# Score triangles cut in halves of 32 queries, two quarters sharing one column, in a windowed-attention and MLP-mixer kernel

## The chip, the cores and the metric

The kernel runs on one core of a Trainium2 chip. Its time is the device time of that core in microseconds (us); of several runs the median is given. Engines are named as the profile names them: PE is TensorE (matmuls; PEld its weight loads), DVE is VectorE, ACT is ScalarE, POOL is GpSimd, SP is SyncE, which here only issues DMAs.

## The reference

One block of a network on a sequence of S = 2048 tokens with D = 512 features, all in bfloat16. `c` is a vector of 512; its modulation gives six vectors of 512. Shortened:

```python
sa, ca, ga, sb, cb, gb = (silu(c) @ w_mod).reshape(6, 512)
h = layernorm(x) * (1 + ca) + sa
q, k, v = split(h @ wqkv)                  # 32 heads of 16 features
s = q @ k.T * 16 ** -0.5                   # per head
mask = (i - j >= 0) & (i - j < 256)        # query i, key j
o = softmax(where(mask, s, -1e9)) @ v
x = x + ga * (o @ wo)
h = layernorm(x) * (1 + cb) + sb
u = gelu(layernorm(h).T @ w1 + b1)         # the MLP mixes tokens: 2048 -> 1792
x = x + gb * (u @ w2 + b2).T               # 1792 -> 2048
```

A query sees itself and the 255 keys before it.

## The kernel before, in words

**Groups, units, chunks.** The sequence is worked through in four groups of 512 tokens (G = 0 to 3). A group's tokens are normalized, transposed and projected to queries, keys and values; a group has two halves of 256 queries (`HQ`). A unit is one half with one set of eight heads (`g8`, four sets); there are 32 units. Keys lie in blocks of 64 (`KB`). A half of 256 queries needs four key blocks before it (-4 to -1) and its own four (0 to 3). Key blocks 0 to 3 are each partly cut off by the diagonal, -4 to -1 partly by the window's far edge; in each, one triangle of 64 x 64 is half in use, and the mask sets the other half to zero.

**A chunk** is one set of score banks of 512 columns: PE writes scores of four head pairs side by side into four PSUM banks (`pss` with three, `psb` with one), ACT takes the exponential of both in two instructions (`et`), DVE multiplies the triangles in `et` by a mask (`maskt`). A tuple `(kb, qs, nq, col)` says: key block `kb`, from query block `qs` on, `nq` query blocks, to column `col`. Two units make a pair of five chunks: near and far for the first, one shared chunk with both units' rest (`MID`), near and far for the second. There are 14 pairs, and for the first half of the sequence four chunks `FIRST` and one `MID_FIRST`: 75 chunks in all. When all chunks of a unit are masked, PE forms the sums (`po`): per piece the values (`VT`) and, with a matrix of small constants (`ones_bd`), the denominators. ACT takes the logarithm and the exponential of minus it (`lz`), DVE multiplies (`OT`).

**Heads two by two.** Scores of two heads come out of one matmul: partition 0 to 63 hold 64 keys of the even head, 64 to 127 the same keys of the odd head. For that the keys stand in `KT` twice, each time with the other head's features set to zero (`split`, with `mask_par`), and the values in `VT` in two halves with zeros beside them.

**Values.** In group 0 the value projection writes each parity of heads straight to its partitions, in matmuls of 256 columns (`v` within `proj0`), and a copy with `mask_half` places them. In groups 1 to 3 it is a plain projection; one copy goes to `vb`, two DMAs on SP swap partition halves into `vs` (`e_vx`), and copies of 64 partitions place them in `VT` (`e_vp`, once for its own half, once for the swapped). `VT[1]` is zeroed by a memset at the start, `VT[2]` by two DMAs.

**The order.** Each step is an `Op` with its engine, and `ORDER` lists the 1,165 operations by number in the order of emission; every engine works its share strictly in that order. `CHOSEN` names the engine of those that may run on more than one. PE switches between four score matmuls side by side (tiles of 32 x 128), four narrow ones for sums (128 x 32) and whole ones (128 x 128). `run_schedule` marks dense work that stands close to sums to be done in 128 x 32 as well (`tiled`, through `mm`).

**The rest.** Between the chunks the order puts the projections of the next group, the output projection and normalizations of the last one (`post`), and parts of the token MLP as soon as a group's normalized tokens `hb` are there (`partials`, evicted to `part`). When attention has ended, `tail` does what is left of the first MLP matmul (`pu`, 56 pieces), and the last loop the second one (`py`), with its outputs.

Of the kernel before, what the change touches and what calls it, by code (L numbers as in the profile page):

```python
# [13 lines left out]
P = 128  # L14
S = 2048
# [8 lines left out]
KB = 64  # L24
HQ = 4 * KB
# [91 lines left out]
]  # L117
CHOSEN = {
    "ACT": [
        47, 48, 50, 51, 74, 82, 1062,  # L120
    ],
    "DVE": [
# [5 lines left out]
    ],  # L128
    "POOL": [
# [86 lines left out]
def kernel(  # L216
# [31 lines left out]
    class Ordered:  # L248
        def __init__(self, engine):
            self.engine = engine  # L250

        def __getattr__(self, name):
            call = getattr(self.engine, name)

            def wrapped(*args, **kwargs):
                ins = call(*args, **kwargs)  # L256
                if pinned[0]:
                    tc.keep_in_program_order(ins)
# [1176 lines left out]
```

## Time and profile before

| | |
|---|---|
| median of 3 runs | 253.28 us (252.91 to 253.66) |
| span of the profiled execution, first to last instruction | 252.3 us |
| time of the profiled execution outside its span | not on the page; the median stands 0.98 us above the span |
| PE busy | 235.3 us (93%), 3949 matmuls, 3949 weight loads |
| DVE busy | 205.4 us (81%) |
| ACT busy | 179.5 us (71%) |
| POOL busy | 126.3 us (50%) |
| granted clock of PE | 1.000 |

The page gives for each engine how long some instruction of it ran. Matmuls overlap, and the end of one is modelled, so a busy PE isn't a PE at its full rate. The line of tenths shows how the shares change over the span. In the groups of instructions a row reads: line, engine, operation, output<-inputs, shapes, count | busy us, mean ns of one | idle time before. The program records all through one wrapper, so all rows have line L256, and groups are told apart by the tiles' names. In the timeline a row reads: start us, length us, engine, line, operation, names, shape, count.

### The profile page before, as it was taken

To read this page: it belongs to the slowest core of one execution; us is meant where nothing else is said; L and a number is where in the kernel's file an instruction comes from. 1 tells how busy PE (TensorE), PEld (TensorE's weight loads), DVE (VectorE), ACT (ScalarE), POOL (GpSimd) and SP (SyncE) were. 2 spreads that over 40 slices of the span, in tenths; PEclk is the share of its full clock that TensorE was granted. 3 is DMA by queue.
4 is the path that set the end of the run, shared out by engine and by line. 5 is a ranking of instruction groups with operands and counts; after the bars stand their busy time and mean duration, and the time that the engine had idled before them with its cause. 6 is when DMAs were issued, how large, how long until landed. Compare 5 with 4: busy or idle time off the path is not lost.

```text
span 252.3 us, 9189 instructions
## 1 busy us (share of the span) xinstructions
PE 235.3 (93%) x3949; PEld 126.0 (50%) x3949; DVE 205.4 (81%) x408; ACT 179.5 (71%) x254; POOL 126.3 (50%) x228
## 2 busy tenths in 40 slices
PE   7988888899987889999999999999999999999995
PEld 2656644445554544555546454556444444444443
DVE  5499998989989998999897999999978764444443
ACT  4699998999999999999999999997147510000000
POOL 8268968795899989845886348173000000000000
PEclk9999999999999999999999999999999999999999
DMA  6999364356055200003401536314999201111111
GB/s 200 323 351 294 48 47 86 44 70 187 3 74 112 53 23 3 4 3 104 131 3 45 155 82 189 105 44 113 343 388 386 108 22 43 44 52 52 42 44 42
DMA packets 42625, 28.13 MB, mean 111 GB/s; under 512 B 12376, under 2 KB 38488, under 8 KB 42584
## 3 DMA queue, kind: packets, MB, share of 16 engines
q1 hardware_dynamic: 42576, 27.54, 39.4%
q8 instruction: 31, 0.51, 0.9%
q14 instruction: 10, 0.08, 0.1%
q10 hardware_dynamic: 8, 0.00, 0.0%
HBM read 22.03 MB, written 2.10 MB: 96 GB/s over the span
## 4 chain that ended last, share of the span: by engine, by line
PE 52%; ACT 24%; DVE 7%; DMA 5%; issue 5%; POOL 4%; SPq 1%; POOLq 0%; DVEq 0%
ACT et L256 20%; PE py L256 19%; PE pu L256 16%; PE po L256 5%; PE pss L256 5%; ACT lz L256 3%; PE pa L256 3%; DMA x<-in_A_x_dram 2%; DVE et L256 2%; DMA h1T<-xn 2%; DMA wmod<-in_w_mod_dram 1%; POOL h1T L256 1%; PE pq L256 1%; DVE st L256 1%; PE pk L256 1%
## 5 line engine op out<-in xcount | busy, mean ns | idle before, releaser
L256 ACT ACTIVATE et<-pss 128x1536 bf16<-128x1536 f32 x75 | 110.7, 1476 | 2.8 <-PE psb L256 2.3
L256 PE MATMUL py<-guT,w2r 128*128 128x512 bf16 (+2 forms) x238 | 48.7, 366 | 0.0
L256 ACT ACTIVATE et<-psb 128x512 bf16<-128x512 f32 x75 | 46.9, 626 | 0.0
L256 DVE TENSOR_TENSOR et<-et,maskt 128x1024 bf16<-128x1024 bf16 (+2 forms) x79 | 46.4, 603 | 0.1
L256 PE MATMUL pu<-hb,w1s 128*32 128x512 bf16 (+1 forms) x302 | 39.0, 380 | 0.2 <-DVE QT L256 0.2
L256 PEld LDWEIGHTS <-w2r 128*128 128x128 bf16 x238 | 22.8, 98 | 26.1 <-issue 0.3
L256 PE MATMUL pss<-QT,KT 32*128 32x64 bf16 (+3 forms) x720 | 29.9, 230 | 6.2 <-ACT et L256 3.5
L256 PE MATMUL po<-et,VT 128*32 128x64 bf16 (+3 forms) x960 | 32.2, 234 | 1.3 <-DVE kb L256 0.6
L256 PE MATMUL po<-et,ones_bd 128*32 128x256 bf16 (+3 forms) x624 | 31.7, 268 | 0.0
L256 PEld LDWEIGHTS <-KT 32*128 32x128 bf16 x960 | 17.1, 92 | 28.5 <-issue 24.6
L256 DVE TENSOR_TENSOR otile<-py,xr 128x512 bf16<-128x512 f32 (+2 forms) x17 | 11.2, 660 | 24.4 <-PE py L256 24.2
L256 POOL TENSOR_SCALAR KT<-kb,mask_par 128x512 bf16<-128x512 bf16 (+1 forms) x36 | 25.0, 707 | 11.4 <-DVE kb L256 11.1
L256 PE MATMUL psb<-QT,KT 32*128 32x64 bf16 (+3 forms) x240 | 29.3, 231 | 0.0
L256 PEld LDWEIGHTS <-VT 128*32 128x32 bf16 x960 | 20.8, 96 | 13.2 <-issue 4.7
L256 PE MATMUL pk<-h1T,wqkv 128*32 128x512 bf16 (+4 forms) x228 | 21.1, 340 | 2.4 <-DVE OT L256 1.0
L256 DVE BATCH_NORM_STATS2 st<-x 128x6 f32<-128x512 bf16 x32 | 21.5, 680 | 2.1 <-DMA x<-in_A_x_dram 2.1
L256 PEld LDWEIGHTS <-wqkv 128*32 128x32 bf16 (+1 forms) x350 | 15.3, 96 | 12.7 <-issue 4.7
L256 PEld LDWEIGHTS <-w1s 128*32 128x32 bf16 (+1 forms) x302 | 14.1, 97 | 15.0 <-issue 1.5
L256 PE MATMUL pv<-wqkv,h1T 128*32 128x512 bf16 (+2 forms) x202 | 17.1, 348 | 1.3 <-DVE OT L256 0.7
L256 PE MATMUL pu<-hb,w1r 128*128 128x512 bf16 (+1 forms) x96 | 17.9, 380 | 0.0
L256 PE MATMUL pa<-wod,OT 128*32 128x512 bf16 (+1 forms) x136 | 17.2, 381 | 0.0
L256 PEld LDWEIGHTS <-ones_bd 128*32 128x32 bf16 x624 | 15.8, 97 | 0.1
(109 smaller groups left out, 350.1 us busy)
## 6 DMA issues: line engine op xcount, KB each, us to landing
w2r<-in_B_w_dram SPq DMA_DIRECT2D x14, 512.0 KB, 10.2
w1s<-in_B_w_dram SPq DMA_DIRECT2D x19, 256.0 KB, 4.0
w1r<-in_B_w_dram SPq DMA_DIRECT2D x9, 256.0 KB, 4.3
x<-in_A_x_dram SPq DMA_DIRECT2D x16, 128.0 KB, 5.2
wmod<-in_w_mod_dram SPq DMA_DIRECT2D x4, 512.0 KB, 7.8
out_dram<-otile SPq DMA_DIRECT2D x15, 128.0 KB, 1.7
wmod<-in_w_mod_dram SPq DMA_DIRECT2D x4, 256.0 KB, 3.9
wqkv<-in_A_wqkv_dram SPq DMA_DIRECT2D x4, 256.0 KB, 5.7
```

The lines of the kernel that those rows point to most:

```text
L256: ins = call(*args, **kwargs)
```

## The change

**Half blocks of 32 queries (`QB`).** Pieces are counted in 32 queries instead of 64. The triangles of 64 x 64 are cut where only one half block of queries can see something, so that pieces have 7, 1, 5, 3 or 2 half blocks and the four key blocks of a near or far chunk fill it exactly.

**The shared chunk.** What is left of a unit are, of each of its eight key blocks, 32 queries with 32 keys. For query block `qb` these are the first 32 keys of block `qb` with its first 32 queries (`side` 0) and the last 32 keys of block `qb - 4` with its last 32 queries (`side` 1). The two are now written to different partition halves of the same 32 columns (`score`): 128 columns per unit instead of 256, 256 per shared chunk instead of 512. Both exponentials of it read 256 columns per bank. Its mask runs twice over them: once with one mask into columns 256 to 511, once with the other in place; each pass keeps one side's half of the partitions. The sums of it are eight pieces of 32 columns per unit for the values, and one matmul over 256 columns in a strided view for the denominators.

**Partitions by key half and head.** For this the 128 partitions of a chunk hold: 32 keys even head, the same 32 odd head, the next 32 even, odd. `KT`, `ones_bd`, `mask_half` and the masks follow that layout.

**Values without swaps.** All value projections write with four matmuls of 32 output partitions (`values`), so the DMAs through `vs` go; `place` puts each half into `VT` in one instruction of 128 partitions that writes the zeros too, so the memset and the two DMAs of zeros go. The operations stay in the list as empty ones, so the numbers in `ORDER` keep their meaning. `vb` has three buffers instead of two.

**New order.** `ORDER` is replaced. Counted by its operations: score and other PE work stand in 158 runs of one class instead of 159; changes of tile shape are 162 instead of 158; the first of the scores and the tail begin with the same PE work, one partial-product piece has moved into the tail. `CHOSEN` changes 37 operations: 17 go from DVE to POOL (two `m2`, four `n2`, four `hb`, three `xn`, one `kk`, two `vo`, one `h1T`), 13 from POOL to DVE (four `n2`, two `hb`, one `m2`, two `h1T`, three `vo`, one `vp`), six from DVE to ACT (five evictions `pe` and one `qe`) and one from ACT to DVE (`ke`). In `Ordered` each instruction gets a tie to the one before it on its engine, without a semaphore.

```diff
-FIRST = [(3, 3, 1, 0), (0, 0, 4, 64), (1, 1, 3, 320)]
-NEAR = [(-1, 0, 4, 0), (0, 0, 4, 256)]
-FAR = [(-2, 0, 3, 0), (3, 3, 1, 192), (-4, 0, 1, 256), (1, 1, 3, 320)]
-MID_FIRST = [(2, 2, 2, 0)]
-MID = [(-3, 0, 2, 0), (2, 2, 2, 128)]
+FIRST = [(3, 6, 2, 0), (0, 0, 8, 64), (1, 2, 6, 320)]
+NEAR = [(-1, 0, 7, 0), (3, 7, 1, 224), (-4, 0, 1, 256), (0, 1, 7, 288)]
+FAR = [(-2, 0, 5, 0), (2, 5, 3, 160), (-3, 0, 3, 256), (1, 3, 5, 352)]
+MID_FIRST = [(2, 4, 4, 0)]
...
-        chunks.append((piece_list(a, NEAR), 0, 512, [(192, 128, 1, 512, 0)]))
-        chunks.append((piece_list(a, FAR), 0, 512, [(128, 128, 2, 128, 0)]))
-        chunks.append((piece_list(a, MID) + piece_list(b, MID, 256), 0, 512, [(64, 128, 2, 256, 0)]))
...
+        near, far = [(192, 64, 2, 64, QB)], [(128, 64, 2, 192, QB)]
+        chunks.append((piece_list(a, NEAR), 0, 512, near))
+        chunks.append((piece_list(a, FAR), 0, 512, far))
+        chunks.append(([(a, None, 0, 0, 0), (b, None, 0, 0, 128)], 0, 256, None))
...
-        1: [op("z", "POOL", 3.45, lambda e: po.memset(VT[1][:], 0.0), ready=2.0, pos=-22.0)],
+        1: [op("z", "POOL", 0.0, lambda e: None, pos=-22.0)],
...
+    def values(dst, h1T, tb, n):
+        wv = wqkv[:, :, 2 * D : 3 * D].rearrange("p j (a two d) -> p j two a d", two=2, d=DH)
+        for dc in range(ND):
+            for r in range(4):
+                tok = tb * P + n * KB + r // 2 * QB
+                te.matmul(
+                    dst[QB * r : QB * (r + 1), n, :].rearrange("p (a d) -> p a d", d=DH),
+                    lhsT=h1T[:, dc, tok : tok + QB], rhs=wv[:, dc, r % 2, :, :],
+                    start=(dc == 0), stop=(dc == ND - 1), tile_position=(0, QB * r), skip_group_check=True,
+                )
+
+    def place(eng, dst, src, tb, half):
+        eng.tensor_scalar(
+            out=dst[:, 2 * tb : 2 * tb + 2, :, half * DH : (half + 1) * DH],
+            in0=src[:].rearrange("p i (a d) -> p i a d", d=DH),
+            scalar1=mask_half[:, half : half + 1], scalar2=0.0, op0=ALU.mult, op1=ALU.add,
+        )
...
-            def e_vx(e):
-                vs = box["vs", tb] = work.tile([P, 256], BF, name="vs", tag=vs_tag, bufs=1)
-                dma.dma_start(out=vs[0:KB, :], in_=box["vb", tb][KB:P, 0, :])
-                dma.dma_start(out=vs[KB:P, :], in_=box["vb", tb][0:KB, 1, :])
...
+                for unit, kb, qs, nq, col in pieces:
+                    if kb is not None:
+                        score(unit, kb, QB * qs, QB * nq, col)
+                    else:
+                        for qb in range(4):
+                            for side in range(2):
+                                score(unit, qb - 4 * side, KB * qb + QB * side, QB, col + QB * qb, side)
...
+                if masks is None:
+                    src = et_of[i][:, :, 0:256].rearrange("p j (n s) -> p j n s", s=QB)
+                    for m0, dst in ((0, et_of[i][:, :, 256:512].rearrange("p j (n s) -> p j n s", s=QB)), (3 * QB, src)):
+                        msk = m[:, m0 : m0 + QB].unsqueeze(1).unsqueeze(1).to_broadcast([P, 4, 8, QB])
+                        ve.tensor_tensor(out=dst, in0=src, in1=msk, op=ALU.mult)
+                    return
...
+                if kb is None:
+                    for side in range(2):
+                        for qb in range(4):
+                            value(0, qb - 4 * side, KB * qb + QB * side, QB, col + 256 * side + QB * qb)
+                    for j in range(4):
+                        te.matmul(
+                            unit["ps"][32 * j : 32 * j + 32, 1, :].rearrange("p (b h k) -> p h b k", b=4, h=2),
+                            lhsT=ones_bd[:],
+                            rhs=et_of[c][:, j, :].rearrange("p (h n k) -> p h n k", h=2, k=QB)[:, :, col // QB : col // QB + 4, :],
+                            start=False, stop=True, tile_position=(0, 32 * j), skip_group_check=True,
+                        )
+                    continue
```

More of the change, by code (lines that the diff above doesn't have):

```diff
@@ L24 @@
 KB = 64
+QB = 32
 HQ = 4 * KB
@@ L250, in __init__ @@
             self.engine = engine
+            self.last = None
         def __getattr__(self, name):
@@ L258, in wrapped @@
                     tc.keep_in_program_order(ins)
+                    if self.last is not None:
+                        tc.add_manual_dep(
+                            ins.ins, self.last, mybir.DependencyInfo(mybir.DependencyClass.NoSync, mybir.DependencyReason.DATA),
+                            reason="order",
+                        )
+                    self.last = ins.ins.name
                 return ins
@@ L289 @@
     nc.gpsimd.memset(mask_half[:], 0.0)
-    nc.gpsimd.memset(mask_half[0:KB, 0:1], 1.0)
-    nc.gpsimd.memset(mask_half[KB:P, 1:2], 1.0)
+    for r in range(4):
+        nc.gpsimd.memset(mask_half[QB * r : QB * (r + 1), r % 2 : r % 2 + 1], 1.0)
     modFM = const.tile([P, 8], F32, name="modFM")
@@ L300 @@
     wod = const.tile([P, ND, D], BF, name="wod")
-    maskt = const.tile([P, 3, KB], BF, name="maskt")
+    maskt = const.tile([P, 5, QB], BF, name="maskt")
     ones_bd = const.tile([P, 2 * DH], BF, name="ones_bd")
     nc.gpsimd.memset(ones_bd[:], 0.0)
-    nc.gpsimd.memset(ones_bd[0:KB, 0:DH], ZSCALE)
-    nc.gpsimd.memset(ones_bd[KB:P, DH : 2 * DH], ZSCALE)
+    for r in range(4):
+        nc.gpsimd.memset(ones_bd[QB * r : QB * (r + 1), r % 2 * DH : (r % 2 + 1) * DH], ZSCALE)
     nothing = const.tile([P, D], BF, name="nothing")
@@ L316 @@
     QT = [[kvpool.tile([P, D], BF, name=f"QT{r}_{g}") for g in range(ND)] for r in range(2)]
-    KT = [[kvpool.tile([P, 8, 2, KB], BF, name=f"KT{r}_{g}") for g in range(ND)] for r in range(3)]
+    KT = [[kvpool.tile([P, 8, 2, 2, QB], BF, name=f"KT{r}_{g}") for g in range(ND)] for r in range(3)]
     VT = [kvpool.tile([P, 8, DH, 2 * DH], BF, name=f"VT{r}") for r in range(3)]
@@ L812, in e_v @@
                     box["v", tb] = bank([P, 2, 256], F32, "pv")
-                wv = wqkv[:, :, 2 * D : 3 * D].rearrange("p j (a two d) -> p j two a d", two=2, d=DH)
-                tok = slice(tb * P + n * KB, tb * P + (n + 1) * KB)
-                for dc in range(ND):
-                    for par in range(2):
-                        te.matmul(
-                            box["v", tb][KB * par : KB * (par + 1), n, :].rearrange("p (a d) -> p a d", d=DH),
-                            lhsT=h1T[:, dc, tok], rhs=wv[:, dc, par, :, :],
-                            start=(dc == 0), stop=(dc == ND - 1), tile_position=(0, KB * par),
-                        )
+                values(box["v", tb], h1T, tb, n)
             def e_ve(e):
@@ L828, in e_vp @@
                 for half in range(2):
[L829 to L835 removed]
+                    place(ENGINE[e], VT[0], box["vb", tb], tb, half)
+            vb_tag = turn("vb", 3)
             a, z = dense("v", [0.5] * 2, e_v, hs[tb // 2], pos, cls="V", alloc="od", ready=W_READY[4])
@@ L974, in e_v @@
                 if n == 0:
-                    box["v", tb] = bank([P, D], F32, "pv")
-                for dc in (2 * n, 2 * n + 1):
-                    mm(
-                        box["v", tb][:], h1T[:, dc, tb * P : (tb + 1) * P], wqkv[:, dc, 2 * D : 3 * D],
-                        (dc == 0), (dc == ND - 1),
-                    )
-            def e_ve(e):
-                vb = box["vb", tb] = work.tile([P, 2, 256], BF, name="vb", tag=vb_tag, bufs=1)
-                copy(
-                    e, vb[:].rearrange("p two (a d) -> p a two d", d=DH),
-                    box["v", tb][:].rearrange("p (a two d) -> p a two d", two=2, d=DH),
-                )
-            def e_vx(e):
-                vs = box["vs", tb] = work.tile([P, 256], BF, name="vs", tag=vs_tag, bufs=1)
-                dma.dma_start(out=vs[0:KB, :], in_=box["vb", tb][KB:P, 0, :])
-                dma.dma_start(out=vs[KB:P, :], in_=box["vb", tb][0:KB, 1, :])
-            def e_vp(e, own):
-                for half in range(2):
-                    rows = slice(KB * half, KB * half + KB)
-                    block, src = (half, box["vb", tb][rows, half, :]) if own else (1 - half, box["vs", tb][rows, :])
-                    ENGINE[e].tensor_copy(
-                        out=VT[r3][rows, 2 * tb + block, :, half * DH : (half + 1) * DH],
-                        in_=src.rearrange("p (a d) -> p a d", d=DH),
-                    )
-            vb_tag, vs_tag = turn("vb"), turn("vs")
+                    box["v", tb] = bank([P, 2, 256], F32, "pv")
+                values(box["v", tb], h1T, tb, n)
+            def e_ve(e):
+                box["vb", tb] = work.tile([P, 2, 256], BF, name="vb", tag=vb_tag, bufs=1)
+                copy(e, box["vb", tb][:], box["v", tb][:])
+            vb_tag = turn("vb", 3)
             war = [av_ops[G - 2, g] for g in range(ND)] if G >= 2 else []
@@ L1008, in v @@
             a.frees = [ve_op]
-            vx = op("vx", "SP", 1.05, e_vx, deps=[ve_op], pos=pos, extra=0.1)
-            own = op("vo", {"POOL": 0.78, "DVE": 0.45}, 0.78, lambda e: e_vp(e, True), deps=[ve_op] + war + zeros[r3], pos=pos)
-            b = op("vp", {"POOL": 0.78, "DVE": 0.45}, 0.78, lambda e: e_vp(e, False), deps=[vx] + war + zeros[r3], pos=pos)
-            slot(vb_tag, ve_op, own, vx)
-            slot(vs_tag, vx, b)
-            v_done[G, tb] = [own, b]
+            vx = op("vx", "SP", 0.0, lambda e: None, deps=[ve_op], pos=pos, extra=-2.0)
+            placed = [
+                op(("vo", "vp")[half], {"POOL": 0.78, "DVE": 0.45}, 0.78,
+                   lambda e, half=half: place(ENGINE[e], VT[r3], box["vb", tb], tb, half), deps=[ve_op] + war, pos=pos)
+                for half in range(2)
+            ]
+            slot(vb_tag, ve_op, *placed)
+            v_done[G, tb] = placed
         for n, pos in sorted(p_at.items(), key=lambda f: f[1]):
@@ L1168, in e_s, with score @@
                 box["sb", i] = ps_b.tile([P, D], F32, name="psb")
[L1169 to L1172 removed]
+                def score(unit, kb, q, width, col, side=None):
+                    block = 4 * unit["H"] + kb
+                    own = KT[block // 8 % 3][unit["g8"]]
+                    q += (unit["H"] % 2) * HQ
+                    part = slice(0, P) if side is None else slice(KB * side, KB * (side + 1))
                     for j in range(4):
                         rows = slice(32 * j, 32 * j + 32)
[L1175 removed]
+                        dst = box["sa"][part, j, col : col + width] if j < 3 else box["sb", i][part, col : col + width]
                         te.matmul(
[L1177 to L1180 removed]
+                            dst, lhsT=own[rows, block % 8, :, :, :] if side is None else own[rows, block % 8, side, :, :],
+                            rhs=QT[unit["G"] % 2][unit["g8"]][rows, q : q + width],
+                            start=True, stop=True, tile_position=(32 * j, part.start), skip_group_check=True,
+                        )
+                for unit, kb, qs, nq, col in pieces:
[5 more added lines that the diff above has]
+                                score(unit, qb - 4 * side, KB * qb + QB * side, QB, col + QB * qb, side)
             def e_ea(e, i=i, lo=lo, hi=hi):
```

90 lines of the change are left out of this document (40 added, 50 removed), and 123 rows, old and new, of tables (CHOSEN, ORDER).

## The prediction

> **What bounds the kernel now.** The page first: its head, the row of busy times, and the busy tenths in 40 slices of 6.3 us.
>
> ```profile
> span 252.3 us, 9189 instructions
> PE 235.3 (93%) x3949; PEld 126.0 (50%) x3949; DVE 205.4 (81%) x408; ACT 179.5 (71%) x254; POOL 126.3 (50%) x228
> PE   7988888899987889999999999999999999999995
> DVE  5499998989989998999897999999978764444443
> ACT  4699998999999999999999999997147510000000
> ```
>
> The slices show two regimes. From slice 2 to slice 27 ScalarE (ACT) is full and VectorE (DVE) nearly so; after that ACT is almost empty and TensorE (PE) alone is full. The shares of the whole span (PE 93%, ACT 71%) hide this, so the second view is the table of windows, cut where the timeline has the first score matmul (10.78 us) and the end of the last group of sums (174.75 us). I call the first row the attention stage, the second the tail.
>
> ```profile
> 10.78:174.75 163.97, 151.94 (x3518) 87.06 (x3517) 153.42 (x300) 160.53 (x219) 119.26 (x201) 1.00 0.39 92
> 174.75:252.30 77.55, 74.73 (x366) 34.41 (x358) 46.58 (x90) 13.49 (x24) 0.00 (x0) 1.00 0.38 134
> ```
>
> Columns: length, busy PE, PEld, DVE, ACT, POOL, granted clock, DMA share, GB/s. In the stage ACT is busy 160.53 of 163.97 us, 98%; DVE 94%; POOL 73%; the clock is 1.00 throughout. The view of waits agrees: who waits for scores or for ACT's reading of them waits little, because the two keep each other just fed.
>
> ```profile
> PE pss L256 <- ACT et L256: 3.5, 12, 0.5
> ACT et L256 <- PE psb L256: 2.3, 5, 0.7
> POOL VT L256 <- DMA vs<-vb: 3.0, 2, 2.3
> ```
>
> So the stage is ACT's, and the tail is a fixed string of PE work. PE's busy time in the stage is no measure of its need. Rows of the timeline give that:
>
> ```profile
> 169.47 0.39 PE L256 MATMUL po<-et,ones_bd 128*32 128x256 bf16 x8
> 169.87 0.26 PE L256 MATMUL pss<-QT,KT 32*128 32x192 bf16 x3
> ...
> 169.95 0.21 PE L256 MATMUL pss<-QT,KT 32*128 32x64 bf16 x3
> ...
> 169.98 0.21 PE L256 MATMUL pss<-QT,KT 32*128 32x64 bf16 x3
> ...
> 170.01 0.26 PE L256 MATMUL pss<-QT,KT 32*128 32x192 bf16 x3
> ...
> 170.21 0.41 PE L256 MATMUL po<-et,VT 128*32 128x192 bf16 x16
> ...
> 178.34 1.89 PE L256 MATMUL pu<-hb,w1s 128*128 128x512 bf16 x8
> ```
>
> Four score matmuls lie side by side in the array. A 192-column group is followed after 0.08 us, which is 2.4 columns per ns; the 64-column groups follow after 0.03 us. The last group starts at 170.01, streams 0.08 us, and the sums start at 170.21: 0.10 to 0.12 us are lost where the shape of the tiles changes. Counting the stage's work in columns at 2.4 per ns, four narrow ones side by side: scores 75 x 512 (16.0 us), sums 76,800 (32.0), 32 value, 62 key and query, 56 partial-product, 28 output-projection and 8 modulation pieces of 1,024 columns or the same in quarters (186 x 0.427 = 79.4). Sum 127.4 us. The order has some 156 changes of tile shape in the stage; at 0.10 us they are 15.6 us. PE needs 143 us of the 164; some 21 us of its stage is waiting, most of it covered by the modelled ends.
>
> **ACT.** The change halves the columns of the 14 shared chunks (the third of each pair's five): the exponentials read 768 and 256 columns instead of 1,536 and 512.
>
> ```profile
> L256 ACT ACTIVATE et<-pss 128x1536 bf16<-128x1536 f32 x75 | 110.7, 1476 | 2.8 <-PE psb L256 2.3
> L256 ACT ACTIVATE et<-psb 128x512 bf16<-128x512 f32 x75 | 46.9, 626 | 0.0
> L256 ACT ACTIVATE lz<-po 128x256 f32<-128x256 f32 x32 | 13.0, 405 | 0.7 <-PE po L256 0.5 <-DVE OT L256 0.2
> L256 ACT ACTIVATE part<-pu 128x512 f32<-128x512 f32 x1 | 0.6, 600 | 0.0
> ```
>
> The two exponentials give (1476 - 626) / 1024 = 0.83 ns per column; the 256-column row (405 against 414 by that slope) says that the slope holds down there. 1,024 columns less are 0.85 us a chunk, 14 x 0.85 = 11.9 us less. The new assignment brings five evictions of partial products to ACT (5 x 0.60 = 3.0 us); a key copy leaves and a query copy comes, which cancel. ACT's stage: 160.5 - 11.9 + 3.0 = **151.6 us**.
>
> **DVE.** Masks: before, 43 of 1,024 elements and 32 of 512. After, the far chunks' 28 shrink to 512, and the 14 shared chunks take two passes of 1,024 (an upper copy into the empty half, then the lower in place): 29 of 1,024 and 60 of 512. That is 28 x 456 - 14 x 742 = +2.4 us; the rows are of runs of 64 and 128 elements, and runs of 32 are not shown: between no more and, if the rate halved, 50 us x 0.6 = 30 us; I take the rows, to which the new runs are nearest in kind: each is still contiguous.
>
> ```profile
> L256 DVE TENSOR_TENSOR et<-et,maskt 128x1024 bf16<-128x1024 bf16 x43 | 31.8, 742 | 0.1
> L256 DVE TENSOR_TENSOR et<-et,maskt 128x512 bf16<-128x512 bf16 x32 | 14.3, 456 | 0.0
> L256 DVE COPY part<-pu 128x512 f32<-128x512 f32 x13 | 8.8, 678 | 0.3 <-PE pu L256 0.2
> L256 DVE TENSOR_TENSOR h<-h,bc_sb 128x512 bf16<-128x512 bf16 x12 | 6.0, 500 | 0.4
> L256 DVE TENSOR_TENSOR h<-h,bc_cb 128x512 bf16<-128x512 bf16 x12 | 5.4, 448 | 0.9 <-POOL h L256 0.8
> L256 DVE TENSOR_SCALAR hb<-h,rs,nm 128x512 bf16<-128x512 bf16 x4 | 2.5, 627 | 0.0
> L256 DVE TENSOR_SCALAR h<-x,rs,nm 128x512 bf16<-128x512 bf16 x4 | 2.0, 497 | 0.0
> L256 DVE TENSOR_SCALAR xn<-x,rs,nm 128x512 bf16<-128x512 bf16 x3 | 1.9, 631 | 0.0
> L256 DVE TENSOR_SCALAR h1T<-h1T,modFM 128x512 bf16<-128x512 bf16 x4 | 1.5, 426 | 0.0
> L256 DVE TENSOR_SCALAR KT<-kb,mask_par 128x512 bf16<-128x512 bf16 x2 | 1.0, 526 | 0.0
> L256 DVE COPY VT<-vb 64x256 bf16<-64x256 bf16 x4 | 0.9, 216 | 0.0
> ```
>
> The new assignment moves to POOL two modulations of two instructions (2 x 0.95), four hb (2.5), three xn (1.9), four n2 (2.0), one key split (1.05), two value placements (4 x 0.216), one h1T (0.85): 11.1 us off; to ACT the five evictions, 3.4 off. It takes from POOL four n2 (2.0), two hb (1.25), one modulation (0.95), two h1T (1.7), and four value placements, each now one pass of 512 like the split's 526 (2.1): 8.0 on. DVE's stage: 153.4 + 2.4 - 14.5 + 8.0 = **149.3 us**.
>
> **POOL and DMA.** Values now reach both halves of the partitions from TensorE, so 24 swaps through SyncE (48 small DMAs) and the two zero-filling DMAs go, and each placement is one instruction.
>
> ```profile
> L256 POOL COPY VT<-vs 64x256 bf16<-64x256 bf16 x24 | 10.8, 452 | 3.9 <-DMA vs<-vb 3.0
> L256 POOL COPY VT<-vb 64x256 bf16<-64x256 bf16 x20 | 10.2, 511 | 3.5 <-DVE vb L256 2.9
> L256 POOL TENSOR_SCALAR VT<-vb,mask_half 128x512 bf16<-128x512 bf16 x8 | 5.8, 731 | 1.3 <-DVE vb L256 1.3
> L256 POOL MEMSET VT<- 128x4096 bf16 x1 | 3.5, 3517 | 0.1
> ```
>
> 44 copies (21.0 us) become 20 passes of 731 ns (14.6); values aside, 15 operations come from DVE and 9 go to it; six more at 731 ns a pass, one or two passes each, are 4 to 9 us. POOL stays near 119 us of the stage; the 45 us in which it is idle there hide this, and without them the 4 to 9 us would show. The memset that goes (3.5 us) pays for more mask building before the stage. What the 3.0 us of waits for swaps covered is late for nobody: the next wait of POOL is for DVE's value copy.
>
> **PE.** The shared chunk's scores become 64 matmuls of 32 columns in 32x64 tiles, its sums 64 of 32 columns plus 8 of 256; the near chunks get two 32-column pieces each in scores and in sums. With w for one row of four tiles of 32 columns (eight half-wide ones for scores), a pair has 8 steps in the shared scores, 16 in the shared sums and 8 in its near chunks, 32, where before the same work was 512 + 512 + 256 columns, 0.533 us. No row shows 32 columns. From below the column rate gives w = 0.013: 32 x 0.0133 - 0.533 = -0.11 us a pair, -1.5 us in all. From above, a load that hides behind nothing:
>
> ```profile
> L256 PEld LDWEIGHTS <-VT 128*32 128x32 bf16 x960 | 20.8, 96 | 13.2 <-issue 4.7 <-DVE QT L256 0.6
> ```
>
> w = 0.096 gives 2.54 us a pair, +36 us. I take w = 0.03, the 64-column groups, nearest in size and with the same loads, hidden there: 0.43 us x 14 = +6.0 us. The value projections keep their columns. The near sums now also wait for the values of blocks 3 and -4, which the far sums right behind them waited for before, and all sums of a unit start when its three masks are done: nothing. Changes of tile shape go up by four (+0.4), one partial-product piece moves to the tail (-0.4). PE needs 143 + 6 = **149 us**.
>
> A second row bears on w, matmuls of one single column, eight of which start 0.025 us apart ((0.34 - 0.163) / 7, the end being that of one):
>
> ```profile
> 6.06 0.34 PE L256 MATMUL ps_fm<-sT,wmod 128*128 128x1 bf16 x8 [0.43 <-DVE sT L256]
> L256 PE MATMUL ps_fm<-sT,wmod x32: 163/163/177, 6.1 to 7.6; 128*128 128x1 bf16 x32
> ```
>
> The Trainium skill, "TensorE: Matmul & The Clock Gate", section "Wait — 56ns, not 53.3ns?", says that starts never come closer than about 25 ns however few the columns; by that rule, an estimate from the page, the term would be +3.7 us instead of +6.0, and the row with its 25 ns agrees.
>
> **The sum.** Three engines that needed 160.5, 153.4 and 143 now need 151.6, 149.3 and 149. If ACT kept its 98% the stage would be 154.9. Three nearly equal engines with buffers between them will hardly do that; I take 97%, 156.5 us, 7.5 less than 164.0. With 0.4 more in the tail the span is 245.2. The page gives the span alone; the median of the runs, 253.28, stands 1.0 above it, so **246.2 us**.
>
> **The rivals.** *PE takes over* (loads partly shown, w of 0.04 to 0.05): 32 x 0.04 - 0.533 = 0.75 us a pair, PE at 153.5, and at 97% a stage of 158; at 0.05 1.07 us, 158 and 163: 248 to 252.7 us. For it: 32-column loads come twice as thick as any in the profile. Against: in the 64-column rows four loads of 96 ns fit in 0.03 us. The Trainium skill, "TensorEngine Tiling (Array Packing)", section "Restrictions and Gotchas", says that column tiling shuts off the fast load, which would strike the 32x64 scores. Here such a load is bounded by the 96 ns row over two buffers, 0.05.
>
> *Slower: the weight loads don't hide at all.* The place is the shared chunk's sums and scores, the price w = 0.096, 36 us on PE; PE at 179, and 179 / 0.97 is a stage of 184: 274 us. It decides from w about 0.052, where PE reaches 159 and the whole gain is gone. Against it speak the same rows.
>
> *The order eats it*: DVE, at 94% of the stage before, stays at 94%, as every mask, copy and normalization waits in its one queue: 149.3 / 0.94 = 158.8, or with the mask runs 10% dearer (+5) 164: 248.5 to 254 us.
>
> *The columns don't bind*: the exponentials shrink but the stage keeps its 164 us, because chunks are paced by the copies and sums between them: 253.5. Against: ACT has 3.4 us of idle time in the stage.
>
> **How the numbers follow.** Chances: forecast 0.70 (241.3 to 249.5), PE takes over 0.10, order 0.11, no effect 0.03, slower by loads 0.06. A measurement of this kernel tells about 0.3% (0.8 us) from nothing. Faster: 0.70, most of PE's and of the order's cases: 0.84. Same 0.05; slower 0.11. The range: below, ACT at 99% gives a stage of 153.1 and 242.8 us, and the same with the five evictions in ACT's idle time 150.1 and 239.8; I go halfway, 241.3. Above, to the order's and PE's cases, 252.
>
> **What would show it.** The 14 shortened exponentials at about 840 and 415 ns; ACT's stage near 152 and still the fullest; 32-column groups 0.025 to 0.03 us apart; masks at 456 and 742 ns; the end of the sums at 167 to 168 us and a tail of 78 us. PE rows full with ACT waiting for scores, or 32-column groups over 0.05 us apart, would prove me wrong.

## The result, and the profile after

The changed kernel takes 278.28 us (275.96 to 278.98, 4 runs), the kernel before 253.47 us beside it: a ratio of 1.0965 [1.0917, 1.1014]. It is 25 us slower, where 7 us faster was forecast, and 26 us above the end of the range. Medians and ratios here and below leave out the few executions that ran in the chip's slower state. The page of the kernel after, its head, busy times, tenths and instruction packets:

```profile
span 276.6 us, 13144 instructions
PE 249.5 (90%) x5955; PEld 142.9 (52%) x5955; DVE 213.8 (77%) x410; ACT 174.7 (63%) x259; POOL 128.0 (46%) x226
PE   7999889879977899786998999897799999999996
DVE  4599999988989979597877999986875985533543
ACT  4599997888978679793988789896513760000000
q8 instruction: 46, 0.75, 1.1%
```

ACT, which was at 9 nearly all through the stage, is mostly at 7 to 9 now; its work has shrunk, the stage hasn't. PE has 2,006 more matmuls and as many more weight loads. The last line had been this in the page before:

```profile
q8 instruction: 31, 0.51, 0.9%
```

These packets are the program itself, 16 KB each (0.75 MB in 46). PE's matmuls and loads number 11,910 here and 7,898 before, which is 259 and 255 for each packet; I take a packet as 256 of PE's instructions. The table of windows of after, the attention stage and the tail (columns as in the prediction; this stage, and those of e9, e13 and e17 further down, are cut 0.3 us ahead of their first score and last sum):

```profile
11.72:196.89 185.17, 164.77 (x5521) 103.18 (x5522) 162.49 (x304) 155.19 (x224) 121.86 (x184) 0.99 0.29 72
196.89:276.58 79.69, 75.30 (x375) 34.67 (x363) 46.36 (x89) 13.98 (x24) 0.00 (x0) 1.00 0.35 126
```

The stage has grown from 164.0 to 185.2 us, and none of the five engines is full in it; the tail is 2 us longer (one stop of 1.8 us lies there, the `pu` row below). So the loss is a matter of waiting, and the view of waits of after says whose:

```profile
ACT et L254 <- PE psb L254: 14.6, 26, 3.8
ACT lz L254 <- PE po L254: 10.6, 12, 2.1
PE po L254 <- issue: 7.5, 9, 1.5
PE pv L254 <- issue: 4.5, 4, 2.9
PE pu L254 <- issue: 1.8, 1, 1.8
PE pss L254 <- issue: 1.7, 3, 0.9
```

ACT waits for PE (14.6 us for scores, 2.3 before; 10.6 for sums, 0.5 before), and PE waits for "issue", that is for nothing that the profile shows. The view of before has no such row for PE. One of these stops in the timeline of after:

```profile
121.77 0.40 PE L254 MATMUL po<-et,VT 128*32 128x32 bf16 x32
122.00 0.31 PE L254 MATMUL po<-et,ones_bd 128*32 128x256 bf16 x4
122.11 0.63 PE L254 MATMUL pv<-wqkv,h1T 128*32 128x256 bf16 x16
122.67 0.20 PE L254 MATMUL pss<-QT,KT 32*64 32x32 bf16 x3
...
123.15 0.20 PE L254 MATMUL psb<-QT,KT 32*64 32x32 bf16 x1
123.28 0.50 PE L254 MATMUL pv<-wqkv,h1T 128*32 128x256 bf16 x9
126.65 0.43 PE L254 MATMUL pv<-wqkv,h1T 128*32 128x256 bf16 x7 [2.87 <-issue]
```

The nine and the seven are one operation of 16 like matmuls with no wait between them; PE stands in the middle of it for some 3 us. The windows around it:

```profile
119.00:123.00 4.00, 4.00 (x169) 2.65 (x168) 4.00 (x6) 3.91 (x6) 3.84 (x5) 1.00 0.48 140
123.00:127.00 4.00, 1.13 (x48) 0.58 (x46) 2.18 (x4) 1.58 (x4) 3.45 (x4) 0.99 0.24 63
127.00:131.00 4.00, 4.00 (x113) 2.17 (x110) 3.84 (x5) 1.94 (x2) 3.01 (x3) 0.59 0.02 4
```

In the first PE takes 337 instructions in 4 us, 84 per us. In the packets' own records of this trace no two start closer than 3.35 us, at the median they are 3.80 us apart (6.1 before): 256 instructions in 3.35 us are 76 per us at best. A packet came here at 124.09 and had landed at 125.14; the one before it had started at 116.64. By the starts of its instructions PE stands 21 times in the stage for over 0.4 us with no semaphore to wait for, 20.4 us together, and 20 of these stops end 1.26 to 1.56 us after a packet has landed. Before, there is none.

The count of instructions agrees. Up to the stop shown, the trace has 6,840 matmuls and loads of PE, which is 26 x 256 + 184, and the packet that lands during this stop is the 26th. The other 19 stops that end behind a packet come at 256 times the number of packets landed by their end, plus 184 to 188. So PE stands each time at the same place of a packet, and goes on once the next has landed. This is the theory that the runs test: **PE runs out of instructions**. The rival theories are those of the prediction (loads that don't hide, the order, DVE).

### The profile page after: what moved, and what is told of

Its sections match the earlier page's. It is cut to its first block, busy times and chain, and to the rows that moved or that the text cites. A ratio compares the mean times of both kernels' runs of the same rounds, so it can differ in the third digit from the quotient of the medians.

```text
span 276.6 us, 13144 instructions
## 1 busy us (share of the span) xinstructions
PE 249.5 (90%) x5955; PEld 142.9 (52%) x5955; DVE 213.8 (77%) x410; ACT 174.7 (63%) x259; POOL 128.0 (46%) x226
## 4 chain that ended last, share of the span: by engine, by line
PE 74%; DVE 10%; issue 7%; ACT 5%; DMA 2%; SPq 1%; DVEq 0%
PE pu L254 18%; PE py L254 17%; PE po L254 12%; PE pss L254 10%; ACT et L254 5%; PE pa L254 4%; PE pv L254 4%; DVE et L254 4%; PE pk L254 3%; PE pq L254 3%; DMA wmod<-in_w_mod_dram 2%; DVE QT L254 1%; DVE h L254 1%; PE psb L254 1%; DVE OT L254 1%
## 5 line engine op out<-in xcount | busy, mean ns | idle before, releaser
L254 ACT ACTIVATE et<-pss 128x1536 bf16<-128x1536 f32 (+1 forms) x75 | 100.1, 1334 | 18.2 <-PE psb L254 14.6
L254 DVE TENSOR_TENSOR et<-et,maskt 128x512 bf16<-128x512 bf16 (+2 forms) x93 | 55.4, 611 | 2.6 <-ACT et L254 2.1
L254 PE MATMUL po<-et,VT 128*32 128x32 bf16 (+5 forms) x1856 | 37.9, 200 | 7.7 <-issue 5.3
L254 ACT ACTIVATE et<-psb 128x512 bf16<-128x512 f32 (+1 forms) x75 | 41.8, 557 | 0.0
L254 PEld LDWEIGHTS <-KT 32*128 32x128 bf16 (+1 forms) x1856 | 23.7, 98 | 27.7 <-issue 25.1
L254 PE MATMUL pss<-QT,KT 32*64 32x32 bf16 (+7 forms) x1392 | 35.1, 203 | 3.0 <-issue 1.7
L254 PE MATMUL psb<-QT,KT 32*128 32x224 bf16 (+3 forms) x464 | 34.4, 204 | 0.6 <-issue 0.6
L254 POOL TENSOR_SCALAR VT<-vb,mask_half 128x512 bf16<-128x512 bf16 x28 | 22.6, 814 | 10.5 <-DVE vb L254 10.5
L254 PE MATMUL pv<-wqkv,h1T 128*32 128x256 bf16 x512 | 18.4, 274 | 4.6 <-issue 4.5
L254 ACT ACTIVATE lz<-po 128x256 f32<-128x256 f32 x32 | 12.3, 388 | 10.9 <-PE po L254 10.6
```

## The experiments

All were timed against the kernel before on the same chip, whose median there was 253.6 to 254.0 us. I give the median and the ratio. The cuts of code are shortened, and some of their lines say in words what the edit does.

### Which part of the change

**e1**: after, but the chunks of the pairs in the form of before.

```diff
-near, far = [(192, 64, 2, 64, QB)], [(128, 64, 2, 192, QB)]   # and a shared chunk of 256 columns
+NEAR64, FAR64, MID64 in pieces of 64 queries, a shared chunk of 512 columns
```

> All of the changed kernel but its half-block pieces: near, far and shared chunks are cut in blocks of 64 queries as before, shared chunks have 512 columns again. PE has 8,328 instructions (7,900 before, 11,912 changed). Supply (PE stops inside unreleased runs because its instructions come at most 256 in about 3.5 us): the stops of over 0.4 us within a run go, some 31 to 33 instruction packets, 251 to 259 us, ACT again fullest. Order (the new order and assignment lose the time): still 270 us or more. Narrow steps (32-column pieces cost array time beyond their count): 250 to 256 us, as for supply.

260.09 us, 1.0234 [1.0194, 1.0273], with 32 packets: 1 us above the range of supply and 10 us below that of the order.

**e5**: after with the `ORDER` and `CHOSEN` of before.

```diff
-ORDER, CHOSEN = those of after
+ORDER, CHOSEN = those of before
```

> The changed kernel with the order and the assignment of the kernel before: half-block triangles and value projections without swaps stay. 12,104 PE instructions. Supply: no order helps, 275 to 285 us with 46 or 47 packets. Order (the new order or assignment costs the 25 us): 250 to 256 us.

274.85 us, 1.0829 [1.0764, 1.0894], with 47 packets: at the lower end of what supply gave, far from the order's range.

**e6**: both edits of e1 and e5, which leaves the layout and the values without swaps.

> The changed kernel with the order and assignment of before and with triangles of 64 as before: what is left of the change is the partition layout and the values without swaps. 8,520 PE instructions, 33 packets. Supply: enough time for them at some 5.5 us a packet, 252 to 256 us. If the values in quarters cost by themselves: 257 us or more.

253.27 us, 0.9982 [0.9958, 1.0006], with 33 packets. The four corners: the half blocks cost 18 us in the new order (260.1 to 278.3) and 22 in the old (253.3 to 274.9); the new order 7 and 3 us; layout and values nothing that can be told. The loss is the half blocks'.

**e11**: e1 with the engines (`CHOSEN`) of before.

> The changed kernel with triangles of 64 and the engine assignment of before, but the new order: tells the two apart in the 6.8 us between the run with triangles of 64 (260.1) and the run with values alone (253.3). If the assignment costs it (3 us more on ACT, which is full with triangles of 64): 254 to 256 us. If the order: 259 to 262 us.

271.46 us, 1.0682 [1.0611, 1.0754]. Neither expectation holds: the new order with the old engines is 11 us worse than with its own. Order and assignment are one thing here and can't be split.

### Instructions or columns

**e2**: after, its dense work never in quarters (`NEAR_RUN` 7 to 0). **e3**: e2, and the value projections of groups 1 to 3 in whole matmuls. Both keep every piece of 32 columns and take other instructions away.

```diff
-NEAR_RUN = 7
+NEAR_RUN = 0
```

> The changed kernel with dense work never cut in quarters: 672 PE instructions fewer (11,240), all 32-column pieces kept, more changes of tile shape (some 40 at 0.1 us). Supply: 2.6 packets of 256 fewer at 3.6 us each, less the added shape changes: 268 to 274 us. Narrow steps or order: 278 us, or up to 4 us more for the shape changes.

> As the kernel with whole dense work, and the value projections of groups 1 to 3 in four whole matmuls of 512 columns in place of 32 of 256 in quarters; the values then lie in another layout, the work of all other engines is the same. 10,568 PE instructions, 1,344 fewer than the changed kernel, all 32-column pieces kept. Supply: 5 packets fewer, 258 to 266 us. Narrow steps or order: 276 to 282 us.

273.74 us, 1.08 [1.0753, 1.0848], with 44 packets; 266.38 us, 1.0498 [1.0443, 1.0553], with 41. The first lies in supply's range, the second 0.4 us above it, and both outside those of the rivals. Two packets less are 4.5 us, three more 7.4: 2.3 to 2.5 us a packet, and the 32-column pieces are all still there.

**e4, e8**: the kernel before with each score and sum matmul cut into pieces of at most 64, and of at most 128 columns. The same columns, masks, exponentials and order; 67 and 43 packets.

```diff
-te.matmul(dst[:, col : col + n], ...)
+for o in range(0, n, 64): te.matmul(dst[:, col + o : col + min(o + 64, n)], ...)
```

> The kernel before with every score and sum matmul cut into pieces of 64 columns: the same columns in the same order, 17,212 PE instructions instead of 7,900, no piece narrower than those it already had. Supply: about 16,500 instructions in the attention stage, 64 packets of 256 at 3.5 us, 226 us instead of 164: 300 to 320 us. Narrow steps: the 64-column groups ran at 0.028 us for 0.0267 us of columns, some 3 us more: 255 to 258 us. Order: 253 to 256 us.

> The kernel before with every score and sum matmul cut into pieces of at most 128 columns: same columns, same order, 11,004 PE instructions, no piece narrower than 64. Supply: some 10,300 in the stage are 40 packets, 141 us at 3.5 us each, under 164 us on the whole but over it where sums crowd: 256 to 272 us, with stops inside unreleased runs. Otherwise: 253 to 255 us.

355.63 us, 1.4006 [1.3965, 1.4046], and 261.72 us, 1.0312 [1.025, 1.0374]. e8 is where supply put it; e4 went far above what I expected. Its page and its waits:

```profile
PE 269.4 (76%) x8605; PEld 154.3 (44%) x8605; DVE 206.4 (58%) x408; ACT 185.4 (52%) x254; POOL 121.2 (34%) x228
q8 instruction: 67, 1.10, 1.3%
PE po L256 <- issue: 45.6, 28, 4.2
PE pss L256 <- issue: 11.3, 7, 2.4
```

PE waits 57 us for "issue" in two rows where the kernel before has none. The clock may have a part in the rest: its mean was 0.932 in the trace of e4, against 0.988 in after and 1.000 before; how much of the 102 us that makes is not shown. No piece is of 32 columns and no tile of 32 x 64 here, so neither form is needed for the loss; many instructions are enough.

**e9**: after with the shared chunk in few instructions. The scores run in 16 matmuls of 64 columns instead of 64 of 32, the value sums in 16 of 128 instead of 64 of 32 (the keys met are then wrong ones); exponentials, masks, order and the rest are those of after.

```diff
-for qb in range(4):
-    for side in range(2):
-        score(unit, qb - 4 * side, KB * qb + QB * side, QB, col + QB * qb, side)
+for qb in (0, 2):
+    score(unit, qb, KB * qb, KB, col + QB * qb)
...
-for qb in range(4):
-    value(0, qb - 4 * side, KB * qb + QB * side, QB, col + 256 * side + QB * qb)
+value(0, -4 * side, 128 * side, 128, col + 256 * side)
```

> The changed kernel, order and all, with the shared chunk's matmuls widened: its scores in 16 matmuls of 64 columns instead of 64 of 32, its value sums in 16 of 128 instead of 64 of 32. It leaves out the right keys for these scores and sums; columns read by ACT, masks, copies and everything else are the same. 9,224 PE instructions instead of 11,912. Supply: 36 packets, the stops inside runs shrink to a few us, and what is left is the forecast's sum without its missing term: 246 to 254 us. If something else in the change cost the time (masks, new order): above 262 us.

253.99 us, 0.9998 [0.9961, 1.0036], 36 packets: 24 us of the 25 are back, for ten packets again 2.4 us each. The 32-column pieces of the near chunks have stayed.

**e7, e10**: e6 with four of the pairs in half blocks, which stays within the supply on average, and the same with `NEAR_RUN` 0.

> As the kernel with values alone, but four of the 14 pairs (numbers 1, 3, 5, 7) in half-block form, no two of them neighbours: 9,544 PE instructions, 37 packets, exponentials shorter by 4 x 0.85 = 3.4 us. Supply: a pair of 10.9 us then has room for three packets, so the extra one of a pair mostly hides: 249 to 254 us. If half-block work costs in proportion whatever the supply (narrow steps): 4/14 of 25 us more, 258 to 262 us.

> As the kernel with four pairs in half-block form under the old order, with dense work never cut in quarters: 8,680 PE instructions instead of 9,544, some 40 more changes of tile shape at 0.1 us. Supply: 3.4 packets fewer near their limit give 3 to 6 us, the shape changes take 2 to 4 back: 252 to 257 us. If supply doesn't bind at four pairs: 258 to 260 us.

256.25 us, 1.0101 [1.0037, 1.0164], and 258.77 us, 1.0213 [1.014, 1.0285]. Both are above what I expected. In e10 fewer packets (34 against 37) did not help. My reading, which no run shows alone: with the supply no longer short, the changes of tile shape that `NEAR_RUN` saves cost more. A mixture brings nothing.

### Where the forecast gain went

e9 is all but fed (two stops that end behind a packet are left in its stage, 2.2 us together), but it is level with before, not 7 us faster. Its stage and the change from the second to the third group, in the views of windows, groups, and timeline (PE, then DVE, then POOL):

```profile
10.31:174.27 163.96, 151.04 (x4152) 94.04 (x4178) 156.66 (x304) 152.12 (x224) 120.77 (x184) 0.99 0.31 83
80.00:84.00 4.00, 1.26 (x64) 1.02 (x59) 3.93 (x8) 1.51 (x2) 1.92 (x3) 1.00 0.62 160
84.00:88.00 4.00, 4.00 (x99) 2.37 (x92) 4.00 (x8) 2.62 (x4) 4.00 (x5) 0.57 0.02 6
L254 DVE TENSOR_TENSOR et<-et,maskt 128x1024 bf16<-128x1024 bf16 x29 | 23.8, 820 | 0.5
82.81 0.29 PE L254 MATMUL po<-et,VT 128*32 128x128 bf16 x8 [2.74 <-DVE OT L254]
77.91 1.26 DVE L254 TENSOR_TENSOR h<-h,bc_sb 128x512 bf16<-128x512 bf16 x1
79.09 1.37 DVE L254 TENSOR_TENSOR h<-h,bc_cb 128x512 bf16<-128x512 bf16 x1
80.50 1.25 DVE L254 TENSOR_TENSOR h<-h,bc_sb 128x512 bf16<-128x512 bf16 x1
82.35 0.41 DVE L254 TENSOR_TENSOR OT<-po,lz 128x256 bf16<-128x256 f32 x1
77.67 1.22 POOL L254 TENSOR_TENSOR h<-h,bc_sb 128x512 bf16<-128x512 bf16 x1
78.85 1.34 POOL L254 TENSOR_TENSOR h<-h,bc_cb 128x512 bf16<-128x512 bf16 x1
80.26 1.21 POOL L254 TENSOR_TENSOR h<-h,bc_sb 128x512 bf16<-128x512 bf16 x1
```

DVE is the fullest now, 156.66 of 163.96 us. For 2.74 us up to 82.81 PE stands, waiting for an `OT` that is queued on DVE behind these modulations; ACT has 1.5 us of work in four; and the granted clock is 0.57 in the 4 us after. The modulations take 1.25 to 1.37 us on DVE while POOL runs the same kind beside it; the prediction quoted 448 and 500 ns for them. Three theories for the missing gain: DVE's time, PE's own work, or the fixed order with its changes of group.

**e12**: e9 without the second of the two mask passes of a shared chunk (14 x 820 ns less on DVE; wrong keys stay in its lower quarters). **e16**: e12 without one of the four matmuls in each projection of the later groups (part of the sum is missing).

```diff
-for m0, dst in ((0, upper), (3 * QB, src)):
+for m0, dst in ((0, upper),):
```

> As e9 (the changed kernel with the shared chunk in 24 instructions instead of 128), and without the second of the two mask passes of a shared chunk, the one in place: the lower quarters keep the scores of a few wrong keys. 14 passes of 1,024 elements at the 820 ns of e9 are 11.5 us less on DVE; PE and ACT have the work of e9. Theory (once PE is fed, DVE is the bound, busy 157 of e9's 164 us of the stage): DVE falls to 145.6, ACT with 152.4 becomes the fullest, at 97% a stage of 157 and a time of 246 to 249 us. Rival (what is left of the stops between packets, or the chain of scores, exponentials and sums, holds the stage): 252 to 255 us, as e9, with DVE idle more.

> The changed kernel with its shared chunk in few instructions and one mask pass (e12), and the projections of the groups after the first without one of their four matmuls, as in e14: about 8 us less on PE and some 400 instructions fewer, so two packets fewer. If PE's own work and supply hold the relieved changed kernel: 244 to 248 us. If the order (waits of several engines for one another) holds it: 250.5 to 253.5 us.

252.92 us, 0.9946 [0.9914, 0.9977], and 252.63 us, 0.9934 [0.9901, 0.9967]. The mask passes taken from DVE bring some 1 us, which the intervals of e9 and e12 hardly tell from nothing, the 8 us of PE nothing that can be told: both go to the rival. (The shared chunk has 32 score and value matmuls in these kernels, where the expectation says 24.)

**e13, e14, e15, e17, e18** take work from the kernel before, in its own order: from ACT (the forecast's very saving, the shared chunk's exponentials over 256 columns), from PE (the projections as in e16), from both, from ACT and DVE, from DVE (the shared chunk's mask cut to 16 columns).

```diff
+if masks == [(64, 128, 2, 256, 0)]:            # e13, e15: ACT
+    hi, masks = 256, 2 * [(64, 128, 1, 256, 0)]
...
-for dc in (2 * n, 2 * n + 1):                  # e14, e15: PE
+for dc in ((2, 3) if n else (0,)):
...
-[(64, 128, 2, 256, 0)]                         # e17 (with hi = 256), e18: DVE
+[(64, 16, 1, 256, 0)]
```

> The kernel before with less work for ACT alone: the two exponentials of each of the 14 shared chunks read 768 and 256 columns instead of 1,536 and 512, the shared masks run twice over these 256 columns in the two passes of 512 elements (so DVE has 2.4 us more, as in the changed kernel), and the sums read the first 256 columns twice; the scores of the other half are left unused. PE's work and its instructions are those of before. Theory 1 (the forecast's: ACT alone bounds the stage): ACT falls by 11.9 us, the stage to about 155 at 97%, a time of 243 to 248 us. Theory 2 (PE is as full as ACT, its waits are covered by nothing): 250.5 to 254 us, with ACT idle in waits for scores.

> The kernel before with less work for PE alone: of the four matmuls of 512 columns in each query, key and value projection of the groups after the first one is left out (that part of the sum is missing). About 38 pieces at 0.213 us are 8 us less on PE. Theory 1 (ACT alone bounds): 252 to 254 us. Theory 2 (both are full, neither has slack): 250 to 253.5 us, the ACT waits for scores gone. If PE alone were the bound: 245 to 247 us.

> The kernel before with both reliefs, ACT's of e13 and PE's of e14. Theory 1 (ACT alone bounds): as e13, 243 to 248 us, no lower than it by more than a microsecond. Theory 2 (both are full): 243 to 248 us, at least 4 us below e13 and below e14. If DVE holds the stage at its 94% (153.4 + 2.4 us): 251 to 254 us.

> The kernel before with less for ACT, as in e13, and less for DVE: of the mask of each of the 14 shared chunks only 16 of its 256 columns are run (the rest keeps the scores of wrong keys), some 14 x 0.65 = 9 us less on DVE than before. Theory 1 (DVE's one queue, full at 94%, paces the stage, and ACT right behind it): 244 to 248.5 us, at least 4 us below e18. Theory 2 (the order and the changes of group hold the time, whatever engine is relieved): 251 to 255 us, with the stop of PE and ACT near 80 us still there.

> The kernel before with less for DVE alone, as in e17 (about 9 us), and ACT's work as before, 160.5 us in the stage. Theory 1 (DVE and ACT bound it together): 250.5 to 253 us, held by ACT. If DVE alone paced it: 245 to 249 us. Theory 2 (the order): 252 to 255 us.

| work taken from | us | ratio |
|---|---|---|
| ACT (e13) | 256.93 | 1.0109 [1.0054, 1.0165] |
| PE (e14) | 254.04 | 0.9998 [0.9969, 1.0027] |
| ACT and PE (e15) | 256.52 | 1.0114 [1.0045, 1.0183] |
| DVE (e18) | 252.51 | 0.9950 [0.9930, 0.9969] |
| ACT and DVE (e17) | 250.45 | 0.9865 [0.9834, 0.9896] |

Theory 1 of e13, the forecast's own, is not met: with ACT's stage down from 160.5 to 150.6 us the kernel is 3 us slower. But this isn't ACT's relief alone, as DVE has 157.7 us in the stage instead of 153.4, and theory 2's 254 us is exceeded too. e14 lies at the upper edge of theory 1, and e15 fits none of its theories. The stage and the change of group in e13, with three masks of DVE there, then the stages in e17 and in e18 and the change of group in e17:

```profile
11.98:178.57 166.59, 153.44 (x3517) 87.26 (x3518) 157.69 (x315) 150.59 (x220) 119.35 (x201) 0.99 0.35 88
80.00:84.00 4.00, 1.68 (x53) 1.48 (x56) 4.00 (x6) 2.35 (x4) 3.84 (x5) 0.83 0.53 125
84.00:88.00 4.00, 4.00 (x84) 1.78 (x80) 3.90 (x8) 1.88 (x4) 3.88 (x6) 0.74 0.35 93
78.43 3.58 DVE L256 TENSOR_TENSOR et<-et,maskt 128x512 bf16<-128x512 bf16 x3
```

```profile
10.57:170.93 160.36, 150.59 (x3517) 86.39 (x3518) 146.81 (x301) 149.61 (x220) 115.38 (x201) 1.00 0.40 94
10.76:172.80 162.04, 151.45 (x3519) 87.25 (x3519) 147.20 (x300) 160.27 (x219) 115.20 (x201) 1.00 0.39 94
80.00:84.00 4.00, 3.64 (x100) 1.83 (x103) 3.81 (x9) 3.17 (x5) 3.88 (x7) 1.00 0.33 92
```

In e13 DVE is full at the same place, PE and ACT stand, and the clock falls again. Three of its masks of 512 take 3.58 us there, 1.2 us each, with modulations of POOL beside them; the row of before has 456 ns. In e17 ACT and DVE have 149.6 and 146.8 us of work, yet the stage is 160.4: 11 us less on the fullest engine and 7 less on the second bring 3.2 us, between the two theories' ranges.

Two pairs of these runs differ in one relief alone. e18 and e17 have DVE alike (147.2 and 146.8 us): 11 us less on ACT bring 2.1 us. e13 and e17 have ACT alike (150.6 and 149.6 us): 11 us less on DVE bring some 6 us. So neither engine holds the kernel before by itself. Once ACT is relieved, DVE's queue takes the gain away, and with both relieved most of the forecast's gain is still missing. What keeps it is not settled: PE, with its 150.6 us, was not relieved in e17, the stop at 80 us that theory 2 named isn't there (PE is busy for 3.64 of the 4 us), and no run changed the order at 80 us alone. None of the kernels that do all the work is faster than the kernel before; e6 is level with it.

## Why the prediction was wrong

**ACT: right.** The rows of after:

```profile
L254 ACT ACTIVATE et<-pss 128x768 bf16<-128x768 f32 x14 | 11.4, 811 | 5.3 <-PE psb L254 5.1
L254 ACT ACTIVATE et<-psb 128x256 bf16<-128x256 f32 x14 | 5.3, 378 | 0.0
L254 DVE TENSOR_TENSOR et<-et,maskt 128x1024 bf16<-128x1024 bf16 x29 | 26.7, 921 | 0.5
L254 DVE TENSOR_TENSOR et<-et,maskt 128x512 bf16<-128x512 bf16 x60 | 28.3, 483 | 2.1 <-ACT et L254 2.1
L254 PE MATMUL po<-et,VT 128*32 128x32 bf16 x1120 | 18.5, 178 | 5.2 <-issue 4.2 <-DVE OT L254 1.0
```

811 and 378 ns against 840 and 415. ACT's stage is 155.2 us in after and 152.1 in e9, against 151.6.

**DVE: mis-sized.** It has 162.5 us in after and 156.7 in e9, against 149.3. The masks are 26.7 + 28.3 = 55.0 us instead of 48.9, and the modulations dearer too. It isn't the runs of 32: the two passes of 1,024 with nothing beside them on POOL take 689 ns (678 before). The 20 that have POOL's one-input work beside them for over half their time take 945. Above the fastest of its own form each, DVE's two-input work (the TENSOR_TENSOR rows) took 7.7 us more before, 19.4 in after, 14.3 in e9. With the order and the engines of before it is 10.7 (e5), so most of the rise came with the new ones. The assignment that I counted as 11.1 us off DVE put on POOL what slows DVE.

The Trainium skill, "SBUF — State Buffer", section "SBUF: two separate sides", says that a DVE operation with two inputs from SBUF and a GpSimd operation that reads SBUF lock a shared pair of ports against each other. The rows of e9 agree for DVE: its modulations take 1.25 to 1.37 us beside POOL's, and 0.42 alone. For POOL they show little: its modulations take 1.21 to 1.34 us beside those, and 1.16 the one time that DVE has no two-input operation beside it.

**PE: the step that failed.** I turned the whole risk into w, the time of a step of 32 columns. For the sums w was right: the 32 matmuls from 121.77 to 122.00 us are eight steps of 0.029 us, against 0.03. For the shared scores it was half of what a step took: 64 matmuls take 122.67 to 123.15, 0.48 us, against 0.24, which is 3.4 us over 14 chunks. But the term that decided was not in the sum at all: the change brings 4,012 matmuls and loads more, and their supply has a rate. In the stage alone it cost 20 us of stops, and with fewer instructions 24 of the 25 us came back (e9). I had "32-column loads come twice as thick as any in the profile" in front of me and asked only whether they hide, not whether they arrive. *The weight loads don't hide at all* gave 274 us, near the measurement for a reason that isn't the one: a step of w = 0.096 is not there.

**The sum: also failed.** A stage at 97% of its fullest engine was not reached by any kernel in which ACT has the forecast's saving: e9 has 95.5%, e17 93%. (151.6 / 0.97 is 156.3 us, not 156.5.) *The order eats it* gives the stage of 164 us that e9 has, with dearer masks as it says; but 9 us less on DVE bring only some 1 us (e12), so DVE's queue alone doesn't explain it. And "the stage is ACT's" was wrong for before: ACT is 98% busy, yet 11 us less of it are worth 2.1 us (e18 against e17). A count was wrong too, without weight in the sum: the swaps that go are 24 DMAs on the page, not 48.

**The signs.** ACT waiting for scores came, 14.6 us of it, but beside a PE that stands, not one that is full. "32-column groups over 0.05 us apart" came for the shared scores (0.06 us a step of eight) and not for the sums (0.029). 167 to 168 us for the end of the sums is 197.

## What to carry to other kernels

Count a change's instructions per engine, not only its columns and bytes: on PE, where a matmul brings its load with it, hold the count in each stretch against the rate at which instruction packets come, and look for "issue" waits in the middle of like matmuls. An engine at 98% did not hold the time alone where a second one was at 94% in a fixed order: take its work away by itself first and see. When work is moved to POOL, ask what DVE does beside it.

## What the runs showed of the hardware

- Instructions come to PE in packets of 256, never closer than 3.35 us in after and 3.8 us at the median there. Beyond some 75 per us (256 in 3.35 us) PE stands, up to 4.2 us at a time (e4), and in after it did so 20 of 21 times at the same place of a packet. The Trainium skill, "Runtime: NRT & Kernel Launch", section "Instruction fetch mechanics", has the 16 KiB blocks of 256 instructions, and calls the cost of crossing them "mostly hidden". Here it was 20 us in the stage of after, of 277 in all, and by the waits of e4 at least 57 of 354.
- A stop of PE of some 3 us is paid for again: the granted clock was 0.59 in the 4 us after the stop at 123 us of after, and 0.57 after that at 80 us of e9, where it was 1.00 in the 4 us ahead of the stop.
- POOL's operations slow DVE's two-input ones, up to three times (1.26 us against 0.42 for a modulation in e9).
